# Moving the first two conversions of channel weights to the sixth and seventh round of the mixing

## The chip, the cores and the metric

The kernel runs on one core of one Trainium2 chip. Its time is the device time of one execution in microseconds (us); the figure quoted is the median of the runs. The core has five engines that each work through their own list of instructions in order: TensorE (PE in the profile, with its weight loads as PEld), VectorE (DVE), ScalarE (ACT), GpSimd (POOL) and SyncE (SP). SP here issues nearly all transfers (DMA). Engines wait for one another by semaphores. Nothing is reordered at run time, so an instruction that waits holds up all that stand behind it on its engine.

## The reference

The program is three stages in a row: a bucketed attention, a gated product, and a mixing block. The change lies in the third, which computes, for a batch of 2 with 768 positions and 512 channels:

```python
def _moe2_ref(x, w_ch1, w_ch2):
    X = np.fft.fft(x, axis=1)
    X = np.fft.fft(X, axis=2)
    mixed = np.real(X).astype(np.float32)
    u = x + mixed
    mu = np.mean(u, axis=-1, keepdims=True)
    var = np.mean((u - mu) ** 2, axis=-1, keepdims=True)
    un = (u - mu) / np.sqrt(var + 1e-06)
    ch = np.maximum(un @ w_ch1, 0.0) @ w_ch2
    return (u + ch).astype(np.float32)

def reference(**kwargs):
    ...
    attn_out = _attn_ref(**attn_kwargs)
    x = attn_out.transpose(0, 2, 1, 3).reshape(B, S, H * D)
    x = _moe_ref(x=x, **moe_kwargs)
    return _moe2_ref(x=x, **moe2_kwargs)
```

`w_ch1` is 512 x 2048 and `w_ch2` is 2048 x 512, both stored as 64-bit floats.

## The kernel before

The three stages run one after the other on the core: the attention until about 258 us, the gated product until about 284 us, the mixing until about 361 us, and the channel stage (the two products with `w_ch1` and `w_ch2`) to the end. Every fp32 operand of a product is split into a high and a low part, and three products take the place of one.

**The mixing** is the loop at L1201. Its 12 jobs are (batch, half, tile) of 128 positions: two batches, three tiles, two halves (s = 0 the even or cosine part, s = 1 the odd or sine part). The loop runs 14 rounds with i = 0 to 13, and is a software pipeline of three steps:

- `own` (L1100) multiplies job i by `w_out`: 12 matmuls of 512 columns, L1105.
- `along_d` (L1138) multiplies job i-2, turned, by the table of the transform along the channels: L1145, six matmuls of 258 columns, or eight for a cosine part (two of them with `first`). ScalarE copies the sum out (L1148, high part), and VectorE subtracts (L1149, low part).
- `turn` (L1122) transposes the folded job i-1 on TensorE, two transposes (L1126), or three for a cosine part (L1128); ScalarE copies them out (L1133, `ft`), VectorE subtracts (L1134).
- `fold` (L1113) copies job i out of its bank on ScalarE (L1115, `y`) and folds it on VectorE (L1118).

A job with s = 1 and tile 0 has two spans, and is turned and multiplied twice. The first product along d of a round reads the `ft` that ScalarE and VectorE made in the round before. In rounds 0 to 4 the second batch's even and odd parts are also formed (L1002, L1007, L1010). In round 7 `both` (L1180) finishes the first batch: `mixed` (L1151) multiplies the sums by the tables along the positions (L1165, 66 matmuls for a batch), VectorE adds (L1171 to L1176), and POOL forms u (L1186). A half's `mixed` reads the three slots of the sums of its half, high parts first. Rounds 8 to 10 center two tiles of u each on VectorE (`center`, L941, three instructions a tile: L944, L945, L946), and rounds 11 to 13 transpose two tiles each (`u_transpose`, L955: eight transposes of TensorE, two copies of ScalarE, two subtractions of VectorE, L962). After the loop `both` finishes the second batch, and the channel stage follows.

**The channel weights** come as 32 blocks of 128 x 512 64-bit floats, numbered h. `channel_load(h)` (L920) issues the DMA of a block on SP into one of two raw buffers. `channel_split(h)` (L935) converts a block into a high and a low fp32 part by `from64` (L128): VectorE L140, ScalarE L143, VectorE L146, L147, L150 and L151, ScalarE L155, POOL L156 (low part) and ScalarE L163 (high part). These steps form a chain that passes to and fro between the engines. Behind it `channel_split` issues the load of block h+2 into the raw buffer that it has just read. Blocks 0 and 1 are loaded in round 4 of the program's order. Blocks 2 and up are converted in the channel stage (L1259 and L1307 on).

The order on each engine is the order in which the Python code calls the instructions; there is no planner. So where a call stands in the loop decides behind what its instructions wait on VectorE, ScalarE and POOL.

Of the kernel before, what the change touches and what calls it, by code (L numbers as in the profile page):

```python
# [102 lines left out]
def block_kernel(  # L103
# [24 lines left out]
    def from64(words_of, raw, dst_h, dst_l, half=False, parts=P, spare=False):  # L128

        n = raw.shape[1]  # L130
        words = raw.bitcast(I32).rearrange("p (n two) -> p n two", two=2)
        lo, hi = words[:, :, 0], words[:, :, 1]
        a, e, g = (words_of(n, x)[:parts] for x in "aeg")
        b = 4 if half else 3

        def fold(x):
            return x.rearrange("p (c f) -> p c f", c=dst_h.shape[1]) if len(dst_h.shape) == 3 else x

        def s0():
            nc.vector.tensor_scalar(a, hi, 0x7FFFFE00, None, op0=ALU.bitwise_and)  # L140

        def s1():
            nc.scalar.activation(a, a, AF.Relu, scale=8.0, bias=col[:parts, b : b + 1])  # L143

        def s2():
            nc.vector.tensor_scalar(g, hi, 0x1FF, 15, op0=ALU.bitwise_and, op1=ALU.logical_shift_left)  # L146
            nc.vector.scalar_tensor_tensor(g, lo, 17, g, op0=ALU.logical_shift_right, op1=ALU.bitwise_or)  # L147

        def s3():
            nc.vector.scalar_tensor_tensor(a, hi, -(2 ** 31), a, op0=ALU.bitwise_and, op1=ALU.bitwise_or)  # L150
            nc.vector.tensor_scalar(e, a, -(2 ** 23), None, op0=ALU.bitwise_and)  # L151

        def s4():
            if spare:
                nc.scalar.mul(g.bitcast(F32), g, 2.0 ** -35)  # L155
                nc.gpsimd.tensor_tensor(dst_l, fold(g.bitcast(F32)), fold(e.bitcast(F32)), op=ALU.mult)  # L156
            else:
                nc.vector.scalar_tensor_tensor(
                    dst_l, fold(g), 2.0 ** -35, fold(e.bitcast(F32)), op0=ALU.mult, op1=ALU.mult
                )  # L160

        def s5():
            nc.scalar.copy(dst_h, fold(a.bitcast(F32)))  # L163

        return [s0, s1, s2, s3, s4, s5]
# [4 lines left out]
    def run(steps):  # L170
        for x in steps:
            x()
# [747 lines left out]
    def channel_load(h):  # L920

        if h >= 2 * NF:
            return
        f, i = divmod(h, 2)
        fs = slice(f * P, (f + 1) * P)
        r = wraw[h] = wq.tile([P, DM], I64, tag=f"raw{i}", name="raw")
        if i:
            nc.sync.dma_start(r, w_ch2[fs, :])
        else:
            nc.sync.dma_start(r.rearrange("p (c f) -> p c f", c=NC), w_ch1[:, fs].rearrange("(c p) f -> p c f", p=P))  # L930
# [4 lines left out]
    def channel_split(h):  # L935
        if h < 2 * NF:
            f, i = divmod(h, 2)
            run(from64(channel_words, wraw[h], *wch[f][2 * i : 2 * i + 2], spare=True))
            channel_load(h + 2)
# [24 lines left out]
    def mixing(es):  # L964
# [33 lines left out]
        def even_odd(b, c, pv_=None):  # L998

            back = g[b][:, c, S:HS:-1] if pv_ is None else pv_[:, ::-1]  # L1000
            for s in range(2):
                nc.vector.tensor_tensor(  # L1002
                    gts[(s + 2 * c) % len(gts)], g[b][:, c, 0:HS], back, op=ALU.subtract if s else ALU.add
                )

        def part_high(b, s, c):
            nc.scalar.copy(gh[b, s][:, c, :], gts[(s + 2 * c) % len(gts)])  # L1007

        def part_low(b, s, c):
            nc.gpsimd.tensor_tensor(  # L1010
                gl[b, s][:, c, :], gts[(s + 2 * c) % len(gts)], f32(gh[b, s])[:, c, :], op=ALU.subtract
            )
# [87 lines left out]
        def own(b, s, kt):  # L1100
            yp = psum()
            n = 0
            for x, w in ((gh[b, s], wo_h), (gh[b, s], wo_l), (gl[b, s], wo_h)):
                for c in range(NC):
                    nc.tensor.matmul(  # L1105
                        yp, x[:, c, kt * P : (kt + 1) * P], w[c], start=n == 0, stop=n == 3 * NC - 1
                    )
                    n += 1
            return yp
# [3 lines left out]
        def fold(b, s, kt, yp):  # L1113
            y = ys[b, s, kt] = m2.tile([P, DM], F32, tag="y", name="y", bufs=7)
            nc.scalar.copy(y, yp)  # L1115
            for part in (s,) if s == 0 or kt else (0, 1):
                fo = folds[b, s, kt, part] = m2.tile([P, 2 * P], F32, tag="fold", name="fold", bufs=2)
                nc.vector.tensor_tensor(  # L1118
                    fo, yp[:, 1:257], y[:, 511:255:-1], op=ALU.subtract if part else ALU.add
                )  # L1120

        def turn(b, s, kt, part):  # L1122
            n = 2 if part else 3
            pt = bank()
            for i, x in enumerate([folds[b, s, kt, part][:, i * P : (i + 1) * P] for i in range(2)]):
                nc.tensor.transpose(pt[:, i * P : (i + 1) * P], x, ident)  # L1126
            if n == 3:
                nc.tensor.transpose(pt[:, 2 * P : 3 * P], ys[b, s, kt][:, 0:P], ident)  # L1128
            fh, fl = turned[b, s, kt, part] = [
                m2.tile([P, 3, P], F32R, tag=f"f{x}", name="ft", bufs=2)[:, :n] for x in "hl"  # L1130
            ]
            src = pt[:, : n * P].rearrange("p (n t) -> p n t", n=n)
            nc.scalar.copy(fh, src)  # L1133
            nc.vector.tensor_tensor(fl, src, f32(fh), op=ALU.subtract)  # L1134
# [3 lines left out]
        def along_d(b, s, kt, part):  # L1138
            fh, fl = turned[b, s, kt, part]
            ops = [(x[:, i, :], tab[:, part, w, i, :]) for x, w in ((fh, 0), (fh, 1), (fl, 0)) for i in range(2)]  # L1140
            if part == 0:
                ops += [(x[:, 2, :], first) for x in (fh, fl)]
            pa = psum()
            for n, (x, w) in enumerate(ops):
                nc.tensor.matmul(pa[:, :NL], x, w, start=n == 0, stop=n == len(ops) - 1)  # L1145
            ah, al = sums[b]
            slot = kt if part == s else 3
            nc.scalar.copy(ah[:, part, slot, :], pa[:, :NL])  # L1148
            nc.vector.tensor_tensor(al[:, part, slot, :], pa[:, :NL], f32(ah)[:, part, slot, :], op=ALU.subtract)  # L1149
# [30 lines left out]
        def both(b, kt):  # L1180

            pm = [mixed(b, s, kt) for s in range(2)]
            for s in range(2):
                total(b, s, kt, pm[s])
            for t, op in ((kt, ALU.add), (3 + kt, ALU.subtract)):
                nc.gpsimd.tensor_tensor(u[b][:, t, :], ys[b, 0, kt], ys[b, 1, kt], op=op)  # L1186
# [10 lines left out]
        def spans(job):  # L1197
            b, s, kt = job
            return [(b, s, kt, part) for part in ((s,) if s == 0 or kt else (0, 1))]

        for i in range(len(jobs) + 2):  # L1201
            if i < len(jobs):
                yp = own(*jobs[i])
            if i > 1:
                for x in spans(jobs[i - 2]):
                    if x[0] not in sums:
                        sums[x[0]] = [m2.tile([P, 2, 4, NL], F32R, tag=y, name="a") for y in ("ah", "al")]
                    along_d(*x)
            if 0 < i <= len(jobs):
                for x in spans(jobs[i - 1]):  # L1210
                    turn(*x)
            if i == 7:
                both(0, 0)
                both(0, 1)
            if i < len(jobs):
                fold(*jobs[i], yp)
            if 0 < i < 5:
                for s in range(2):
                    part_high(1, s, i - 1)
                    part_low(1, s, i - 1)  # L1220
            if i < 4:
                even_odd(1, i)
            elif i == 4:
                gs.close()
                late_tiles()
                channel_load(0)
                channel_load(1)
            elif i == 7:
                both(0, 2)
            elif 8 <= i < 11:  # L1230
                for t in (i - 8, i - 5):
                    center(0, t)
                if i > 8:
                    channel_split(i - 9)
            elif i > 10:
                for x in range(2):
                    u_transpose(0, 2 * (i - 11) + x, psum)
# [3 lines left out]
    with ExitStack() as es:  # L1241
        mixing(es)
# [125 lines left out]
```

## Time and profile before

| | us |
|---|---|
| median of 3 runs | 638.09 (637.91 to 639.32) |
| the profiled execution, its own time | 639.26 |
| span of the profiled execution, first to last instruction | 637.5 |
| busy in the span: TensorE matmul | 618.5 (97%) |
| busy in the span: VectorE | 446.6 (70%) |
| busy in the span: ScalarE | 356.6 (56%) |
| busy in the span: POOL | 263.6 (41%) |
| mean granted TensorE clock (1 is full) | 0.995 |

The rows below are of that profiled execution; all times in them count from the start of its span. Busy matmul time is modelled, as matmuls are pipelined. The granted clock is the share of full speed that the chip allowed TensorE. A timeline row has the start, the duration, the engine, the line and the operation, output before input; in square brackets stands how long the engine was idle before it, and which engine's work ended that idle time. The chain of waits follows the work that ended last backwards, at each step to what released it.

### The profile page before, as it was taken

How to read it: one execution, taken by the hardware profiler on the slowest of the kernel's cores; microseconds unless marked ns; L12 is line 12 of the kernel's file. 1: busy time of each engine (PE TensorE's matmuls, PEld its weight loads, DVE VectorE, ACT ScalarE, POOL GpSimd, SP SyncE). 2: the span in 40 equal slices, each digit the busy share in tenths (PEclk: the TensorE clock that was granted, in tenths of full speed). 3: DMA queues.
4: the chain of work that ended last, by engine and by line, in shares of the span. 5: the costliest groups of instructions: out<-in, count | busy, mean ns of one | idle time of the engine just before them, and what ended most of it. 6: DMA issues, size and time to landing. Idle time of an engine off the chain costs nothing.

```text
span 637.5 us, 10561 instructions
## 1 busy us (share of the span) xinstructions
PE 618.5 (97%) x3794; PEld 578.1 (91%) x3794; DVE 446.6 (70%) x847; ACT 356.6 (56%) x713; POOL 263.6 (41%) x289
## 2 busy tenths in 40 slices
PE   7999999999999999999996999999999999999997
PEld 6899999999999998998895889999998999999996
DVE  4998989898989997897468788888885511111113
ACT  5887989898988897735325255555665110111221
POOL 7133577777888697873141433333331000000000
PEclk9999999999999999999998999999999999999999
DMA  6957475747747520261002044443440200000002
GB/s 155 197 127 178 117 185 125 163 121 161 169 117 184 145 65 10 70 244 48 0 2 67 1 133 133 132 133 122 125 130 21 100 1 1 0 1 1 1 1 99
DMA packets 54060, 60.25 MB, mean 95 GB/s; under 512 B 28936, under 2 KB 42332, under 8 KB 53752
## 3 DMA queue, kind: packets, MB, share of 16 engines
q1 hardware_dynamic: 53272, 56.02, 33.5%
q0 software_dynamic: 432, 3.55, 1.5%
q8 instruction: 30, 0.49, 0.3%
q14 instruction: 22, 0.18, 0.1%
q10 hardware_dynamic: 304, 0.01, 0.0%
HBM read 33.98 MB, written 3.15 MB: 58 GB/s over the span
## 4 chain that ended last, share of the span: by engine, by line
PE 86%; DVE 8%; ACT 2%; issue 1%; DMA 1%; POOL 0%; SPq 0%; DVEq 0%; ACTq 0%; POOLq 0%
PE pf L1275 20%; PE acc L1287 20%; PE sp L537 10%; PE op L597 9%; PE ptp L574 8%; PE ps L1105 4%; PE ps L216 3%; PE ps L1165 3%; PE bp L414 2%; PE ps L1145 2%; DVE ptl L586 2%; DVE sd L549 2%; PE late L216 1%; PE ptp L669 1%; PE ptp L649 1%
## 5 line engine op out<-in xcount | busy, mean ns | idle before, releaser
L1287 PE MATMUL acc<-w,hid 128*128 128x512 f32 x576 | 137.0, 390 | 0.0
L1287 PEld LDWEIGHTS acc<-w,hid 128*128 128x128 f32 x576 | 107.4, 188 | 19.7
L1278 DVE SCALAR_TENSOR_TENSOR hid<-pf,hid 128x384 fp32r<-128x384 f32 x60 | 32.3, 556 | 120.0 <-ACT hid L1277 120.0
L549 DVE TENSOR_SCALAR_CACHE_REDUCE sd<-sp 128x768 f32<-128x768 f32 x96 | 91.0, 949 | 14.7 <-PE sp L537 13.8
L1275 PE MATMUL pf<-uth,w 128*128 128x384 f32 x480 | 94.7, 338 | 0.3 <-POOL w L156 0.3
L586 DVE TENSOR_TENSOR ptl<-ptp,pth 128x768 fp32r<-128x768 f32 x96 | 91.5, 953 | 3.2 <-ACT pth L582 3.2
L537 PE MATMUL sp<-qk 128*128 128x384 f32 x384 | 90.9, 359 | 2.8 <-DVE sd L549 1.7
L582 ACT CAST pth<-ptp 128x768 fp32r<-128x768 f32 x96 | 77.3, 806 | 26.8 <-PE ptp L574 10.0
L556 ACT ACTIVATE sd<-sd,nm 128x768 f32<-128x768 f32 x96 | 90.7, 945 | 2.7 <-DVE sd L549 2.7
L1277 ACT ACTIVATE hid<-pf 128x384 fp32r<-128x384 f32 x60 | 28.0, 488 | 113.8 <-PE pf L1275 113.8
L1275 PEld LDWEIGHTS pf<-uth,w 128*128 128x128 f32 x480 | 85.6, 187 | 3.1 <-POOL w L156 0.6
L156 POOL TENSOR_TENSOR w<-cv 128x512 fp32r<-128x512 f32 x32 | 41.3, 1292 | 99.8 <-DVE cv L151 86.8
L574 PE MATMUL ptp<-ident,sd 128*128 128x128 f32 x576 | 78.6, 272 | 0.2 <-ACT sd L556 0.2
L597 PE MATMUL op<-ptl,v 128*128 128x256 f32 x288 | 73.6, 285 | 0.3 <-DVE ptl L586 0.3
L597 PE MATMUL op<-pth,v 128*128 128x256 f32 x288 | 73.5, 281 | 0.2 <-ACT xc L610 0.2
L537 PEld LDWEIGHTS sp<-qk 128*128 128x128 f32 x384 | 62.4, 189 | 6.5 <-DVE sd L549 4.3
L574 PEld LDWEIGHTS ptp<-ident,sd 128*128 128x128 f32 x576 | 65.9, 141 | 1.1 <-ACT sd L556 0.5
L615 POOL TENSOR_TENSOR xm<-xc,xs 64x256 f32<-64x256 f32 x48 | 35.5, 741 | 70.7 <-DMA xs<-xc 28.9
L597 PEld LDWEIGHTS op<-ptl,v 128*128 128x128 f32 x288 | 54.1, 188 | 1.7 <-DVE ptl L586 0.5
L597 PEld LDWEIGHTS op<-pth,v 128*128 128x128 f32 x288 | 54.1, 188 | 0.5 <-ACT xc L610 0.4
L143 ACT ACTIVATE cv<-cv,col 128x512 int32<-128x512 int32 x32 | 23.2, 725 | 53.5 <-DVE cv L140 53.5
L1275 PE MATMUL pf<-utl,w 128*128 128x384 f32 x240 | 52.1, 338 | 0.0
(214 smaller groups left out, 1050.7 us busy)
## 6 DMA issues: line engine op xcount, KB each, us to landing
raw<-in_moe_w_ch_dram SPq DMA_DIRECT2D x32, 512.0 KB
qk<-ht SPq DMA_DIRECT2D x60, 192.0 KB
qk<-lt SPq DMA_DIRECT2D x30, 192.0 KB
rqk<-in_q_dram SPq DMA_DIRECT2D x16, 192.0 KB
rqk<-in_k_dram SPq DMA_DIRECT2D x16, 192.0 KB
rv<-in_v_dram SPq DMA_DIRECT2D x8, 384.0 KB
out_dram<-o SPq DMA_DIRECT2D x12, 256.0 KB
xs<-xc SPq DMA_DIRECT2D x47, 64.0 KB
```

Source lines behind the costliest of these rows:

```text
L156: nc.gpsimd.tensor_tensor(dst_l, fold(g.bitcast(F32)), fold(e.bitcast(F32)), op=ALU.mult)
L537: nc.tensor.matmul(sp[:, a, :HS], q2[i][:, m, qi * P : (qi + 1) * P], k2[i][:, m, a * HS : (a + 1) * HS], start=m == 1, stop=m == 0,)
L549: nc.vector.tensor_scalar(sd[n].rearrange("p (a c) -> p a c", a=2), sp[:, :, :HS], CLAMP, None, op0=ALU.min, op1=ALU.min, accum_out=st[p][ ...
L556: nc.scalar.activation(sd[n], sd[n], AF.Exp, bias=st[p]["nm"][:, i : i + 1], scale=-1.0, accum_out=st[p]["sums"][:, i : i + 1],)
L574: nc.tensor.transpose(tp[:, r // 3, c0 : c0 + P], sd[n][:, r * P : (r + 1) * P], ident)
L582: nc.scalar.copy(p_parts(n)[0], tp)
L586: nc.vector.tensor_tensor(lo, tp, f32(ho), op=ALU.subtract)
L597: nc.tensor.matmul(po[kb], v3[:, r, c0 : c0 + P], pt[kb][x][:, r, :], start=r == 0 and x == 0, stop=r == R - 1 and x == 1,)
L615: add[kb] = lambda: nc.gpsimd.tensor_tensor(st[p]["xm"][mr, blk * QB : (blk + 1) * QB], xc[mr, :], xs[mr, :], op=ALU.add)
L1275: nc.tensor.matmul(pf[:, :HS], w[:, c, :], x[:, c, cs], start=n == 0, stop=n == 3 * NC - 1)
L1278: nc.vector.scalar_tensor_tensor(hl[:, cs], pf[:, :HS], 0.0, f32(hh)[:, cs], op0=ALU.max, op1=ALU.subtract)
L1287: nc.tensor.matmul(acc, x[:, ts_], w, start=f == 0 and n == 0, stop=f == NF - 1 and n == 2)
```

## The change

Two lines leave the branch for rounds 8 to 10, in which rounds 9 and 10 converted blocks 0 and 1, and a branch for rounds 5 and 6 is added that converts the same two blocks. Both places are at the end of their round.

```diff
--- before.py
+++ after.py
@@ -1230,8 +1230,8 @@
             elif 8 <= i < 11:
                 for t in (i - 8, i - 5):
                     center(0, t)
-                if i > 8:
-                    channel_split(i - 9)
+            elif 5 <= i < 7:
+                channel_split(i - 5)
             elif i > 10:
                 for x in range(2):
                     u_transpose(0, 2 * (i - 11) + x, psum)
```

Nothing else differs. The matmuls on TensorE and the DMAs on SP stand in the same order as before.

ScalarE, rounds 5 to 7, as a difference (the three added rows are one conversion; `cv` is its scratch, `w_0_4335` and `w_0_4337` are high parts of the channel weights, `ft` the turned job, `a` the sums, `y` the job):

```order
 L1133 CAST ft<-pw 128x384
 L1115 COPY y<-ps 128x512
+L143 ACTIVATE cv<-cv,col 128x512
+L155 ACTIVATE cv<-cv 128x512
+L163 CAST w_0_4335<-cv 128x512
 L1148 CAST a<-ps 128x258
 L1133 CAST ft<-pw 128x256
 L1115 COPY y<-ps 128x512
+L143 ACTIVATE cv<-cv,col 128x512
+L155 ACTIVATE cv<-cv 128x512
+L163 CAST w_0_4337<-cv 128x512
 L1148 CAST a<-ps 128x258
```

The two conversions now stand behind the copy `y` of rounds 5 and 6, and ahead of the copies of the sums and of `ft` of the next round.

ScalarE, rounds 9 to 11, as a difference:

```order
 L1133 CAST ft<-pw 128x384
 L1115 COPY y<-ps 128x512
-L143 ACTIVATE cv<-cv,col 128x512
-L155 ACTIVATE cv<-cv 128x512
-L163 CAST w_0_4335<-cv 128x512
 L1148 CAST a<-ps 128x258
 L1133 CAST ft<-pw 128x256
 L1115 COPY y<-ps 128x512
-L143 ACTIVATE cv<-cv,col 128x512
-L155 ACTIVATE cv<-cv 128x512
-L163 CAST w_0_4337<-cv 128x512
```

The copies of the sums and of `ft` of rounds 10 and 11 now follow the copy `y` of the round before directly.

VectorE at the end of round 9, as a difference (`mu_4323` and `u_4322` are the mean and the u of the first batch, `raw` the block as loaded):

```order
 L945 BN_AGGR mu_4323<-st 128x2
 L946 TENSOR_SCALAR u_4322<-u_4322,mu_4323 128x512
-L140 TENSOR_SCALAR cv<-raw 128x512
-L146 TENSOR_SCALAR cv<-raw 128x512
-L147 SCALAR_TENSOR_TENSOR cv<-raw,cv 128x512
-L150 SCALAR_TENSOR_TENSOR cv<-raw,cv 128x512
-L151 TENSOR_SCALAR cv<-cv 128x512
 L1149 TENSOR_TENSOR a<-ps,a 128x258
 L1134 TENSOR_TENSOR ft<-pw,ft 128x256
```

Behind the centering of the second tile of the round now stands the low part of the sums of round 10, with no conversion between. On POOL the two products L156 move ahead of the additions L1186 that form u for the first batch.

## Rows read from the trace of the kernel before

**Rows 1.** The page's slices, 15.9 us each: TensorE's granted clock in tenths, and bytes moved.

```profile
PEclk9999999999999999999998999999999999999999
...
GB/s 155 197 127 178 117 185 125 163 121 161 169 117 184 145 65 10 70 244 48 0 2 67 1 133 133 132 133 122 125 130 21 100 1 1 0 1 1 1 1 99
```

**Rows 2.** Waits, 323 to 362 us: who <- for whom, total us, times, longest us.

```profile
PE ps L1145 <- ACT ft L1133: 5.1, 2, 4.5
```

**Rows 3.** Stretches: length, busy us (count) of PE, PEld, DVE, ACT, POOL, then clock.

```profile
344.00:348.00 4.00, 1.16 (x5) 1.16 (x6) 3.37 (x8) 3.66 (x8) 1.28 (x1) 0.59 0.34 118
348.00:350.00 2.00, 2.00 (x11) 2.00 (x10) 1.66 (x4) 1.00 (x3) 0.00 (x0) 0.50 0.10 35
350.00:352.00 2.00, 2.00 (x13) 2.00 (x13) 1.25 (x3) 1.17 (x2) 0.00 (x0) 0.62 0.00 0
```

**Rows 4.** Chain of waits, 280 to 380 us: start, us, what; around the removed conversions.

```profile
330.48 1.71 PE ps L1145 x14
...
332.62 0.43 DVE a L1149
333.05 0.56 DVE ft L1134
...
333.96 0.61 DVE st L944
...
336.65 0.34 DVE cv L140
...
346.84 2.09 PE ps L1145 x8
...
352.92 7.97 PE ps L1165 x66
```

**Rows 5.** The same chain: TensorE's pieces at full clock.

```profile
306.45 0.72 PE ps L1145 x6
307.18 0.22 PE pw L1126 x2
...
307.50 2.81 PE ps L1105 x12
310.31 0.98 PE ps L1145 x8
...
352.05 0.87 PE ps L958 x8
```

**Rows 6.** Timeline, rounds 5 to 7: start, us, engine, line, operation; idle before it.

```profile
308.54 0.42 DVE L1118 TENSOR_TENSOR fold<-ps,y 128x256 f32<-128x256 f32 x1
...
311.32 0.38 ACT L1148 CAST a<-ps 128x258 fp32r<-128x258 f32 x1 [2.81 <-PE ps L1145]
...
312.50 0.42 DVE L1118 TENSOR_TENSOR fold<-ps,y 128x256 f32<-128x256 f32 x1
...
315.07 0.38 ACT L1148 CAST a<-ps 128x258 fp32r<-128x258 f32 x1 [2.60 <-PE ps L1145]
...
316.54 1.26 PE L1165 MATMUL ps<-a,seq 128*128 128x258 f32 x9
...
318.54 0.42 DVE L1171 TENSOR_TENSOR y<-y,ps 128x257 f32<-128x257 f32 x1 [1.06 <-PE ps L1165]
```

**Rows 7.** Timeline: first conversion in round 9, its start and what follows it.

```profile
336.56 0.42 DVE L140 TENSOR_SCALAR cv<-raw 128x512 int32<-128x512 int32 x1
...
339.21 0.37 ACT L1148 CAST a<-ps 128x258 fp32r<-128x258 f32 x1
339.25 1.27 POOL L156 TENSOR_TENSOR w<-cv 128x512 fp32r<-128x512 f32 x1 [11.79 <-DVE cv L151]
```

**Rows 8.** Timeline of SP's queue: issue of the first two raw channel blocks.

```profile
284.25 0.38 SPq L930 DMA_DIRECT2D raw<-in_moe_w_ch_dram  x1
284.68 0.51 SPq L928 DMA_DIRECT2D raw<-in_moe_w_ch_dram  x1
```

**Rows 9.** Timeline, round 11: the pair of VectorE's subtractions for u.

```profile
347.80 1.29 DVE L962 TENSOR_TENSOR utl<-ps,uth 128x512 fp32r<-128x512 f32 x2
```

## The prediction

> **What bounds the kernel now.** I read the profile in this order: the slices of the page, the table of waits for the stretch around the removed conversions, the stretch table with the granted clock, the chain of waits, and the timeline of the rounds that lose or receive a conversion. Round i below is the pass with that index of the mixing loop (i counts from 0, so the change's sixth, seventh, tenth and eleventh rounds are 5, 6, 9 and 10). TensorE is the bound nearly everywhere; the reader is to see the one place where it is not. In the page's slices its clock shows one dip, in the slice that begins near 335 us [rows 1]. The waits of 323 to 362 us put 5.1 us of TensorE's idleness on two waits of L1145 (the products along d) for ScalarE's L1133, 4.5 us of it in one piece [rows 2]. The granted clock then stands at 0.59 in 344 to 348 us and at 0.50, the lower level of 1.2 GHz, in 348 to 350, and averages 0.62 over 350 to 352, so that it is full again only near the end of that stretch [rows 3]. The chain of waits says why: from 332 to 347 us it leaves TensorE and runs through VectorE's products, folds and centerings into the first conversion, on into a further round of the same and into the second conversion, and returns at 346.84 [rows 4]. So the two conversions lie on the path that sets the end, in rounds in which VectorE is already full: without one, round 9 takes VectorE 4.03 us (332.62 to 336.65, [rows 4]), while TensorE needs 2.81 + 0.98 + 0.22 = 4.01 us for a round of one `own`, eight products and two turns [rows 5].
>
> **What is removed from rounds 9 and 10.** A conversion is five VectorE, three ScalarE and one POOL instruction and, behind them, one load issued by SP. From its first instruction at 336.56 to ScalarE's next copy for the mixing at 339.21 it holds that chain for 2.65 us [rows 7]. Nothing in these rounds covers it. What comes next when it is gone has to be followed on both engines, in the chain's times.
>
> TensorE: the products of round 9 end at 330.48 + 1.71 = 332.19 [rows 4]. A turn with three transposes takes 0.32 (307.18 to 307.50), so `own` of round 10 starts at 332.51; 2.81 for it, 0.98 for eight products and 0.22 for a turn of two put round 11 at 336.52. From there at full clock: `own` 2.81, six products 0.72, a turn 0.32, eight transposes of u 0.87, which ends at 341.24; eight products 0.98, a turn 0.22, u 0.87, to 343.31; six products 0.72 and u 0.87 [rows 5]. With no wait the second batch's `mixed` starts at 344.90.
>
> VectorE: round 9 ends at 336.65 as before. Round 10 waits for its products (336.30) and ScalarE's copy of them, about 0.4, so it runs from 336.7 for 4.03, to 340.7. Round 11 is 0.43 + 0.56 + 0.42 and the pair of u subtractions, 1.29 [rows 4, 6, 9], to 343.4; the low parts of the last turn follow 0.43 + 0.56 later, at 344.4. The last six products read them from their fifth matmul, at 343.31 + 4 x 0.12 = 343.8. So about 0.5 us of wait is left, and `mixed` starts at 345.4 instead of 352.92 [rows 4]: **7.5 us** gained. A second route gives the same: 5.1 us of waits [rows 2], plus what the slow clock took, which is 352.92 - 346.84 = 6.08 us for work of 0.98 + 0.22 + 0.87 + 0.72 + 0.87 = 3.66 us at full clock, 2.4 us; together 7.5. Bounds: 8.0 if VectorE never holds TensorE (344.90), and 6.5 if handovers and the trailing VectorE cost another microsecond. I take 7.5.
>
> **What is added to rounds 5 and 6.** Here VectorE has no centering, and from round 5 on no even and odd parts. ScalarE stood idle for 2.81 us ahead of the copy at 311.32 and 2.60 us ahead of the one at 315.07 [rows 6]; this idle time is the cover. In round 5 VectorE is free at 308.54 + 0.42 = 308.96; 2.65 us later, at 311.61, ScalarE turns to the copy that ran at 311.32, 0.29 us late. TensorE's next use of that round's turn is a whole `own` (2.81) later. In round 6 the fold of 312.50 moves to 312.79, VectorE is free at 313.21, and the copy of 315.07 runs at 315.86, ending at 316.24 (it takes 0.38), with VectorE's subtraction ending near 316.7. This is the tight place: `mixed` of the sine half starts at 316.54 and reads the copied slot in its third matmul, at 316.54 + 2 x 0.14 = 316.82, and the low part in its seventh, at 317.38 [rows 6]. 0.6 us of slack remain, so I cost this at nothing; without the cover each conversion would cost up to 2.65 us. VectorE's additions behind it come 0.5 us late and recover in the idle 1.06 us ahead of 318.54 [rows 6]. POOL's two products (1.27 each, [rows 7]) end near 317.2, before the sums for u that start when VectorE's additions are through.
>
> **Loads.** The two raw blocks that the moved conversions read were issued at 284.25 and 284.68 us [rows 8], and the slices show the core's transfers at 0 and 2 GB/s between 303 and 335 us [rows 1], so they have long landed at 308. The loads that each conversion issues behind it move with it, to about 311 and 316, into that quiet stretch and past no other entry of SP's queue; their first reader is the third conversion, behind the mixing. Cost nothing.
>
> **After the mixing.** The third conversion and the first channel matmul are released by the last VectorE addition of the mixing, as before. Everything from `mixed` of the second batch on is tied to that point and not to a fixed time, so the gain should reach the end whole.
>
> **The sum.** The profiled execution took 639.26 us, span 637.5; minus 7.5 that is 631.8, span 630.0. The median of the runs shown is 638.09, 1.17 below the profiled one. Against it: 638.09 - 7.5 = **630.6**.
>
> **Rivals.** (a) *VectorE stays the bound to the end of the rounds.* Its round 12 with u is 0.43 + 0.56 + 1.29 = 2.3 us against TensorE's 2.07, and round 13 is alike; if each handover is 0.2 late and the waits grow to 1.5 to 3 us in rounds 11 to 13, the gain is 5 to 6.5: 631.6 to 633.1. For it: 4.03 against 4.01 leaves no reserve. Against it: round 11 gives VectorE time, since TensorE has 4.7 us there.
>
> (b) *The clock falls anyway.* From 339.3 to the start of `mixed` TensorE would run 5.6 us, of which 3.2 are transposes (three times 0.87, 0.32, 0.22). If such a mix did not hold the clock, up to 5.6 us would be lost again: 636.2. Against it: the clock rose from 0.50 in 348 to 350 us to a mean of 0.62 over 350 to 352, so full by its end, while TensorE ran this very mix of products and u transposes [rows 3]. The Trainium skill, in TensorE: Matmul & The Clock Gate, section Part 4: PE-mode transpose, says that transposes do not count as activity that brings the full clock. By that rule alone the time would lie towards 636; the trace speaks against it as far as these two microseconds go.
>
> (c) *The stall is moved, not removed, and the program becomes slower.* The place is the third matmul of the sine half at 316.82. It decides when the copy of 315.86 comes more than 0.6 us later than I have it. Exposed in full, the two conversions cost 2 x 2.65 = 5.3; if the clock fell there too, the 66 matmuls of `mixed` (7.97 us, [rows 4]) would run at half speed and cost up to 8.0 more. 638.09 - 7.5 + 13.3 = 643.9. The stall alone, without the clock, still leaves a gain: 635.9. It needs both, and ScalarE's idle times speak against either.
>
> (d) *Nothing changes*, because what is won in the mixing is waited for at the start of the channel stage: it would need a transfer or POOL step there that is tied to an absolute time, and I see none. 638.
>
> **How the numbers follow.** The forecast, 630.6 with 629.8 to 631.6 for its own bounds, gets 0.78; (a) 0.10; (b) 0.03; the stall of (c) without the clock 0.02; (c) in full 0.03; (d) 0.04. A difference of 0.2%, 1.3 us, is about what a measurement of this kernel tells from no change. Faster is the forecast, (a), (b) and the half of (c): 0.93; same 0.04; slower 0.03. The range holds the forecast and (a), with some room above for handovers: 629.6 to 633.1.
>
> **What would show it.** Right: L1145 in rounds 11 and 12 no longer waits for L1133; the clock shows no dip in any slice; the second batch's `mixed` starts near 345.4; ScalarE's copies of 311.32 and 315.07 come 0.3 and 0.8 us later and TensorE does not notice; the stretch from `mixed` to the end is as long as before. Wrong: a wait of L1165 for L1148 near 317, a clock dip near 317 or 345, or a new wait at the first channel matmuls.

## The result, and the profile after

The changed kernel takes 631.44 us (631.11 to 631.64, 4 runs) against 638.71 us (637.91 to 639.64, 4 runs) of the kernel before: the ratio is 0.9884, with a 95% interval of 0.9872 to 0.9897, so 7.3 us are gained, 6.6 to 8.2 by the interval. The forecast was 638.09 - 7.5 = 630.6; the difference predicted, 7.5 us, is met within 0.2, and the median lies 0.8 us above the forecast mostly because the median of before was 0.6 us higher this time: its four runs are two pairs, 637.91 and 638.09, 639.32 and 639.64, and the median lies between them. The profiled execution of the changed kernel took 631.46 us. Its trace runs ahead of the trace of before by 0.12 us at the start of round 5 (303.53 against 303.65) and by 0.13 us where `mixed` of the first batch begins (315.23 against 315.36); 0.13 us is to be added to its times where the two are set side by side.

The page of the changed kernel: span, and the granted clock in slices.

```profile
span 629.7 us, 10559 instructions
...
PEclk9999999999999999999999999999999999999999
```

The span is 629.7 us against 637.5, and the slice with the dip of the clock [rows 1] is gone: all 40 stand at 9 tenths or more.

The table of waits of the changed kernel, from 316 us to the first rounds of the channel stage; some of TensorE's rows: who <- for whom, total us, times, longest us.

```profile
PE acc L1275 <- DVE y L1176: 0.9, 1, 0.9
...
PE acc L1275 <- ACT w L163: 0.6, 1, 0.6
...
PE acc L1275 <- POOL w L156: 0.3, 1, 0.3
PEld ps L1145 <- DVE ft L1134: 0.2, 1, 0.2
```

The 5.1 us of L1145 waiting for ScalarE's L1133 [rows 2] are no longer there. What is left of waits in the mixing is a weight load (PEld) that waits 0.2 us for VectorE's low part L1134. The three rows of L1275 belong to the start of the channel stage; the longest of them, 0.9 us for the last addition, was there before too.

The stretches of the changed kernel; the columns are as in [rows 3].

```profile
340.00:344.00 4.00, 3.97 (x35) 3.74 (x33) 3.93 (x9) 3.90 (x9) 0.00 (x0) 1.00 0.00 0
344.00:346.00 2.00, 2.00 (x19) 2.00 (x19) 1.87 (x5) 1.45 (x3) 0.00 (x0) 1.00 0.00 0
346.00:348.00 2.00, 2.00 (x19) 2.00 (x19) 1.30 (x4) 0.00 (x0) 0.00 (x0) 1.00 0.00 0
```

TensorE is busy for 3.97 of 4.00 us in 340 to 344 and the clock is at 1.00 throughout, where before it stood at 0.59, 0.50 and 0.62 [rows 3]. VectorE is no less busy than before in that stretch (3.93 of 4.00): it is full, but almost nothing waits for it.

The chain of waits of the changed kernel through rounds 11 to 13 and the second batch's `mixed`.

```profile
339.17 0.72 PE ps L1145 x6
...
340.22 0.87 PE ps L958 x8
341.09 1.05 PE ps L1145 x8
...
343.24 0.48 PE ps L1145 x4
...
343.75 0.51 PE ps L1145 x2
...
345.13 7.99 PE ps L1165 x66
...
353.15 0.42 DVE y L1171
```

It stays on TensorE from one end to the other, but for a break of 0.03 us ahead of the last two products of round 13. In the chain of before the same addition of VectorE stands here:

```profile
360.91 0.42 DVE y L1171
```

`mixed` of the second batch begins at 345.13, 345.26 in the time of before, against 352.92 [rows 4]: 7.7 us earlier. It takes 7.99 us as before (7.97), and from VectorE's addition at 353.15 to the end of the span are 629.7 - 353.15 = 276.6 us, as before (637.5 - 360.91 = 276.6). Nothing of the gain is lost behind it.

The timeline of the changed kernel in rounds 5 to 7, where the conversions are now.

```profile
311.41 0.37 ACT L1148 CAST a<-ps 128x258 fp32r<-128x258 f32 x1
...
315.56 0.36 ACT L1148 CAST a<-ps 128x258 fp32r<-128x258 f32 x1
...
316.40 1.26 PE L1165 MATMUL ps<-a,seq 128*128 128x258 f32 x9
```

ScalarE's copies L1148 come at 311.41 and 315.56; in the time of before these are 311.54 and 315.69, so they are 0.22 and 0.62 us later than at 311.32 and 315.07 [rows 6]. The sine half starts at 316.40, and TensorE has no wait there. The load behind the second conversion goes out at 315.02, in the quiet stretch.

### The profile page after: what moved, and what is told of

Same layout as the page of the kernel before. It is cut to its first block, busy times and chain, and to the rows that moved or that the text cites. A ratio compares the mean times of both kernels' runs of the same rounds, so it can differ in the third digit from the quotient of the medians.

```text
span 629.7 us, 10559 instructions
## 1 busy us (share of the span) xinstructions
PE 616.0 (98%) x3794; PEld 576.7 (92%) x3794; DVE 445.9 (71%) x847; ACT 356.4 (57%) x713; POOL 263.9 (42%) x289
## 4 chain that ended last, share of the span: by engine, by line
PE 88%; DVE 7%; ACT 2%; issue 1%; DMA 1%; POOL 0%; SPq 0%; DVEq 0%; ACTq 0%; POOLq 0%
PE pf L1275 20%; PE acc L1287 20%; PE sp L537 10%; PE op L597 9%; PE ptp L574 8%; PE ps L1105 5%; PE ps L216 3%; PE ps L1165 3%; PE bp L414 2%; PE ps L1145 2%; DVE ptl L586 2%; DVE sd L549 2%; PE late L216 1%; PE ptp L669 1%; PE ptp L649 1%
## 5 line engine op out<-in xcount | busy, mean ns | idle before, releaser
L1275 PE MATMUL pf<-uth,w 128*128 128x384 f32 x480 | 94.8, 338 | 0.2 <-POOL w L156 0.2
L1275 PEld LDWEIGHTS pf<-uth,w 128*128 128x128 f32 x480 | 85.7, 188 | 2.9 <-POOL w L156 0.6
L156 POOL TENSOR_TENSOR w<-cv 128x512 fp32r<-128x512 f32 x32 | 41.4, 1294 | 89.6 <-DVE cv L151 76.6
L1275 PE MATMUL pf<-utl,w 128*128 128x384 f32 x240 | 52.1, 338 | 0.0
```

The source lines that it names most:

```text
L1275: nc.tensor.matmul(pf[:, :HS], w[:, c, :], x[:, c, cs], start=n == 0, stop=n == 3 * NC - 1)
```

## Experiments

Two theories besides mine were set against each other. **A**: the conversions lay on the chain of VectorE and ScalarE for which TensorE waits, in rounds that VectorE already fills, and the slow clock followed from the wait. **B**: the gain comes from weights and loads being there earlier. **C**: only ScalarE's place behind the conversion matters, not VectorE's work. In the kernels that add lines the line numbers behind them shift by a few; L1145 and L1165 are named by their operation where that happens.

### Only the first conversion moved

```diff
                 for t in (i - 8, i - 5):
                     center(0, t)
-                if i > 8:
-                    channel_split(i - 9)
+                if i == 10:
+                    channel_split(1)
+            elif i == 5:
+                channel_split(0)
```

> Block 0 is converted in round 5, block 1 stays in round 10. Theory A (the two conversions lay on the chain of VectorE and ScalarE that TensorE waits for, in rounds that VectorE fills already, and the slow clock followed from the long wait): round 10 of VectorE ends near 340.5 as in the changed kernel, the conversion then holds ScalarE's next copies to about 343.1, so the products of round 12 wait some 2.8 us instead of 4.5, and there is no wait of 0.6 us in round 11. Gain 4.7 us against the kernel before if the clock stays at full, 3 if it falls. Theory B (the gain comes from weights and loads being there earlier): each block carries its half, gain 3.7, with no link to a wait of L1145. Nothing of the computation is left out.

Measured: 635.68 us, ratio 0.9955 (0.9941 to 0.9970), a gain of 2.7 us. TensorE's timeline around round 12 of this kernel:

```profile
343.93 1.39 PE L1145 MATMUL ps<-tab,ft 128*128 128x258 f32 x6 [2.73 <-ACT ft L1133]
```

the stretch behind it:

```profile
344.00:348.00 4.00, 4.00 (x20) 3.95 (x21) 3.28 (x7) 2.76 (x7) 0.48 (x1) 0.57 0.30 115
```

and the start of `mixed` in its chain:

```profile
349.54 8.00 PE ps L1165 x66
```

The wait is the 2.73 us that theory A gave (2.8), behind the turned sine part, and the clock fell after it, to 0.57 in 344 to 348 us. The 3 us forecast for that case were nearly met. Against the changed kernel 2.73 us of wait are lost, and 1.6 us in the work behind it, a part of which ran at the lower clock: from 343.93 to `mixed` at 349.54 are 5.61 us, where the changed kernel takes 345.13 - 341.09 = 4.04. Theory B gave 3.7 for this half, and it names no such wait.

### Only the second conversion moved

```diff
                 for t in (i - 8, i - 5):
                     center(0, t)
-                if i > 8:
-                    channel_split(i - 9)
+                if i == 9:
+                    channel_split(0)
+            elif i == 6:
+                channel_split(1)
```

> Block 1 is converted in round 6, block 0 stays in round 9. Theory A: the wait of 0.6 us in round 11 and the short one behind it stay, VectorE is 2.65 us late through round 10 and ends it near 343.5, the low parts of the last cosine turn come near 344.5, and the products of round 12 wait 1.5 to 2 us for them, with the clock at full. Gain about 5 us against the kernel before; together with the run that moves block 0 alone more than the 7.3 of both, since the two delays add up on one chain. Theory B: gain 3.7, and the two runs add up to 7.3.

Measured: 633.75 us, ratio 0.9923 (0.9906 to 0.9939), a gain of 4.6 us. TensorE's two waits, and the clock in the stretch behind them:

```profile
339.51 1.03 PE L1145 MATMUL ps<-tab,ft 128*128 128x258 f32 x6 [0.59 <-ACT ft L1133]
...
343.94 0.50 PE L1145 MATMUL ps<-tab,ft 128*128 128x258 f32 x2 [1.52 <-DVE ft L1134]
```

```profile
344.00:348.00 4.00, 4.00 (x34) 3.92 (x35) 3.88 (x9) 2.98 (x7) 0.00 (x0) 1.00 0.02 4
```

The 0.59 us of round 11 are back as in the kernel before, and in round 12 TensorE stops at the fifth of six matmuls for 1.52 us, for VectorE's low part of `ft`, as forecast; the clock stays at 1.00. So one conversion too many in round 9 is felt two rounds later, through VectorE. One expectation failed: the two runs were to add up to more than 7.3 us, and they give 2.7 + 4.6 = 7.3, the sum that theory B had given. I had left out of that sentence that the first of them loses part of its gain to the clock. Against theory B speak the unequal halves, and that the changed kernel takes the same 276.6 us as before from VectorE's addition to the end: nothing was won where the weights are read.

### Both conversions left in rounds 9 and 10, ahead of the centerings

```diff
             elif 8 <= i < 11:
-                for t in (i - 8, i - 5):
-                    center(0, t)
                 if i > 8:
                     channel_split(i - 9)
+                for t in (i - 8, i - 5):
+                    center(0, t)
```

> Both conversions stay in rounds 9 and 10, but stand ahead of the centerings of the round and no longer behind them. Theory A: VectorE has 4.03 + 2.65 us of work in such a round in either order, against 4.0 of TensorE, so the waits change their place (from ScalarE's L1133 to VectorE's low parts, L1134) and are split into several of 0.5 to 2.6 us, 5 us together; the clock may hold, since no single wait is as long as 4.5. Gain 0 to 3 us. Theory C (it is only ScalarE's place behind the conversion that holds TensorE, not VectorE's work): ScalarE is through with its part while VectorE centers, and the gain is 5 us or more.

Measured: 637.92 us, ratio 0.9990 (0.9981 to 1.0000), 0.4 us or nothing. TensorE's waits in this kernel, and its clock:

```profile
340.15 0.50 PE L1145 MATMUL ps<-tab,ft 128*128 128x258 f32 x2 [0.43 <-DVE ft L1134]
...
343.78 0.74 PE L1145 MATMUL ps<-tab,ft 128*128 128x258 f32 x4 [1.82 <-ACT ft L1133]
346.81 0.80 PE L1145 MATMUL ps<-tab,ft 128*128 128x258 f32 x2 [2.29 <-DVE ft L1134]
```

```profile
344.00:348.00 4.00, 1.71 (x9) 1.51 (x9) 3.93 (x9) 1.19 (x3) 0.33 (x1) 0.61 0.29 108
```

The two waits of before, 0.60 and 4.50 us, are now three, 0.43, 1.82 and 2.29 us, 4.5 us together (I had said 5), two of them for VectorE's L1134. ScalarE's copy `ft` of round 11 ends at 343.73 instead of 346.78, 3 us earlier, and it helps nothing, since TensorE then stops until 346.81 for VectorE's low part, as late as before (346.84): theory C falls. The order within the round matters little, the amount of VectorE work in it does. The clock, which I thought might hold, fell to 0.61 in 344 to 348 us, so that little of the 3 us that were possible remained.

### The kernel before, with TensorE kept busy in the wait

```diff
         for i in range(len(jobs) + 2):
             if i < len(jobs):
                 yp = own(*jobs[i])
+            if i == 12:
+                to = psum()
+                for _ in range(30):
+                    nc.tensor.matmul(to[:, :NL], gh[1, 0][:, 0, 0:P], first, start=True, stop=True)
```

> The kernel before with 30 further products of 258 columns at the start of round 12, 3.6 us at full clock, into a bank that nobody reads, in the 4.5 us in which TensorE waited there. They are added work that changes no output. Theory A: TensorE has hardly any idle time left there, the granted clock stays at 1.00 in 344 to 352 us, and the 2.4 us that the slow clock took come back: 636.3 us. If the slow clock costs nothing, or falls all the same: 638.7. That tells how the 7.3 us divide into waits (5.1) and clock (2.4).

Measured: 637.10 us, ratio 0.9982 (0.9972 to 0.9991), a gain of 1.2 us, 0.6 to 1.8 by the interval. The added matmuls and the rest of the wait in the timeline:

```profile
341.79 3.85 PE L1207 MATMUL ps<-first,gh 128*128 128x258 f32 x30
346.53 1.10 PE L1145 MATMUL ps<-tab,ft 128*128 128x258 f32 x6 [0.90 <-ACT ft L1133]
```

The chain from there to `mixed`:

```profile
346.53 1.34 PE ps L1145 x8
...
349.50 0.51 PE ps L1145 x2
...
350.88 8.00 PE ps L1165 x66
```

The clock in the stretches that were slow before:

```profile
344.00:348.00 4.00, 3.10 (x25) 2.84 (x24) 3.41 (x7) 3.66 (x9) 1.28 (x1) 1.00 0.44 129
348.00:350.00 2.00, 1.96 (x17) 1.75 (x16) 2.00 (x6) 1.63 (x4) 0.00 (x0) 1.00 0.01 4
```

The clock stays at 1.00, and the products start where they started before (346.53 is 346.83 in the time of that trace). From there to `mixed` are 350.88 - 346.53 = 4.35 us, against 352.92 - 346.84 = 6.08 before [rows 4]. So the clock cost 1.7 us in the trace, where I had put 2.4. The difference (4.35 against the 3.66 that I had counted) falls into two: the first eight products take 1.34 us behind the wait, not 0.98, and with TensorE fast again the last six wait for VectorE's low parts, which the slow clock had covered (the last two take 0.51 us as in the changed kernel). The median gives still less, 1.2, and the interval just reaches 1.7. The runs of before differ among themselves, too: in 12 of the 19 in this series the mean granted clock is 0.997 and the median time 638.25 us, in 6 it is 0.995, as in the profiled execution, and the median 638.97; the run here lies 1.15 and 1.87 us below these. So what the clock costs differs from run to run. That the clock share is some 1 to 2 us, and the greater part of the gain is the waits, is shown; its exact size is not.

### Each conversion done twice in rounds 5 and 6

On the changed kernel:

```diff
             elif 5 <= i < 7:
+                channel_split(i - 5, False)
                 channel_split(i - 5)
```

Here `False` leaves out the load behind the first of the two.

> The changed kernel with each of the two conversions done twice in its round (5 and 6), the same result written again; the added work changes no output. Theory A (the place in rounds 5 and 6 is free because ScalarE and VectorE have 2.6 to 2.8 us of idle time there and no more; I left 0.6 us of slack in round 7): the second conversion of a round has no cover and also waits for POOL's L156 of the first. TensorE waits 1 to 2 us for L1133 ahead of the products of round 7 and 3 to 5 us in mixed ahead of the sine half, and the clock may fall there: 631.4 + 5 to 9 = 636.5 to 640.5. Rival D (VectorE and ScalarE have far more room there than my 0.6 us, or TensorE does not depend on them so soon): 631.4 to 632.5.

Measured: 640.49 us, against 638.9 us of before on the same chip, ratio 1.0030 (1.0019 to 1.0041); so 9 us more than the changed kernel, at the upper end of what was expected, and slower than the kernel before. The second conversion on VectorE, POOL's product ahead of it, and TensorE's two waits (the lines of the mixing are one higher here):

```profile
311.06 1.29 POOL L156 TENSOR_TENSOR w<-cv 128x512 fp32r<-128x512 f32 x1 [4.49 <-DVE cv L151]
311.15 1.49 DVE L140 TENSOR_SCALAR cv<-raw 128x512 int32<-128x512 int32 x1 [0.23 <-ACT w L163]
...
315.55 1.02 PE L1146 MATMUL ps<-tab,ft 128*128 128x258 f32 x6 [1.76 <-ACT ft L1134]
...
323.28 1.47 PE L1166 MATMUL ps<-a,seq 128*128 128x258 f32 x7 [3.38 <-ACT a L1149]
```

The clock in two stretches behind the waits:

```profile
316.00:320.00 4.00, 3.89 (x21) 3.41 (x19) 3.44 (x8) 1.86 (x3) 1.10 (x2) 0.62 0.37 121
...
324.00:326.00 2.00, 2.00 (x11) 2.00 (x11) 0.86 (x3) 0.00 (x0) 0.19 (x1) 0.50 0.53 203
```

The waits are 1.76 us ahead of the products of round 7 (forecast 1 to 2) and 3.38 us in `mixed` ahead of the third matmul of the sine half, for ScalarE's copy, at the place that the prediction had called the tight one. The clock fell after both, to 0.62 and 0.50. The waits make 5.1 of the 9 us; the rest, of which the slower work behind them is likely a part, was not divided further. So the room in rounds 5 and 6 is real but fits one conversion, not two: rival D falls, and so does the idea that the place in the order hardly matters.

### The first channel matmuls in another pair of banks

The trace of the changed kernel leaves 0.94 + 0.56 + 0.32 us of waits at the start of the channel stage. This is its timeline there: POOL's u, TensorE's first channel matmuls, two instructions of the third conversion, and TensorE's two waits for `w`.

```profile
350.52 6.62 POOL L1186 TENSOR_TENSOR u<-y 128x512 f32<-128x512 f32 x5
...
354.05 1.64 PE L1275 MATMUL acc<-uth,w 128*128 128x384 f32 x8 [0.94 <-DVE y L1176]
354.48 1.51 DVE L146 TENSOR_SCALAR cv<-raw 128x512 int32<-128x512 int32 x1
...
356.03 1.67 DVE L147 SCALAR_TENSOR_TENSOR cv<-raw,cv 128x512 int32<-128x512 int32 x1
...
359.05 0.96 PE L1275 MATMUL acc<-uth,w 128*128 128x384 f32 x4 [0.56 <-ACT w L163]
...
360.33 0.97 PE L1275 MATMUL acc<-uth,w 128*128 128x384 f32 x4 [0.32 <-POOL w L156]
```

The edit, on the changed kernel:

```diff
-            pf = tile_a(2 + 2 * g + a) if g < 2 else tile_f()
+            pf = tile_a(2 + 2 * g + a) if g == 1 else tile_f()
```

> The changed kernel; the first channel matmuls go into the two banks of the pair pf and no longer into acc2 and acc3, so they do not wait for the last addition of the mixing (0.94 us in both kernels). Theory E (the path at that point runs from that addition through the third conversion to w of L1275, and not through TensorE): TensorE starts 0.9 us earlier and waits that much longer for w: 631.4, within 0.3. Rival F (each wait of TensorE counts): 630.5.

Measured: 631.56 us (631.46 to 631.69), ratio to before 0.9886: as the changed kernel.

```profile
352.93 1.56 PE L1275 MATMUL pf<-uth,w 128*128 128x384 f32 x8
...
359.06 0.96 PE L1275 MATMUL acc<-uth,w 128*128 128x384 f32 x4 [1.77 <-ACT w L163]
```

TensorE starts at 352.93 instead of 354.05 and then waits 1.77 us instead of 0.56; it resumes at 359.06 and 360.33, within 0.01 us of where it did. A wait that is not on the path is worth nothing (theory E).

### The VectorE part of the third conversion in round 7

On the changed kernel; `split_front` is `channel_split` up to the scaling of the low word, with the load, and `split_back` the copy and POOL's product of the same block:

```diff
             elif i == 7:
                 both(0, 2)
+                split_front(2)
...
-        channel_split(2)
+        split_back(2)
```

> The changed kernel with the VectorE part and the scaling of the third conversion in round 7, behind both for the first batch, where VectorE stood idle for 2.9 us and ScalarE for 4.6; only the copy and POOL's product of it stay at the start of the channel stage. By the same reasoning as for the first two: covered in round 7 (cost 0), and the waits of 0.56 and 0.32 us of L1275 for w go: 631.4 - 0.9 = 630.5; the 0.94 us behind the last addition stay. If round 7 has no cover, the products of round 8 or 9 wait instead and the time is 631.4 or more.

Measured: 630.51 us (630.19 to 631.58), ratio to before 0.9868: 0.9 us below the changed kernel, as forecast; with the interval, 0.9852 to 0.9885 against 0.9872 to 0.9897, the difference is not clear of the noise. The profiled execution is the slowest of the four (631.58 us). At the start of the channel stage it is about 1.6 us later than the changed kernel: 1.15 us of them it has already at the first batch's `mixed` (316.14 against 314.99), ahead of the moved work. TensorE in round 12 and at the start of the channel stage:

```profile
343.12 0.52 PE L1169 MATMUL ps<-tab,ft 128*128 128x258 f32 x2 [0.39 <-DVE ft L1158]
...
355.63 1.64 PE L1300 MATMUL acc<-uth,w 128*128 128x384 f32 x8 [0.94 <-DVE y L1200]
...
359.91 1.56 PE L1300 MATMUL acc<-uth,w 128*128 128x384 f32 x8
```

The 0.94 us stay, the two waits for `w` are gone. But the cost in round 7 is not 0: TensorE waits 0.39 us in round 12 for VectorE's low part (L1158 here), and the time between the two `mixed` grows by 0.4 us, from 29.90 (314.99 to 344.89) to 30.31 (316.14 to 346.45). In turn the start of the channel stage, from that `mixed` to the first product with `w_ch2`, takes 17.65 us instead of 19.01, 1.4 less, more than the 0.9 of idle time. The forecast of 0.9 was met by two errors that offset each other.

### Both edits

> Both edits. TensorE starts the channel stage 0.94 us earlier and finds w ready or nearly (POOL is busy with u until about 357 and forms the low part then, ready near 358.4, while TensorE wants it near 357.9): 631.4 - 0.9 - 0.5 = 630.0, and 629.5 if both gains are whole. By rival F with the other two runs: the two gains add up.

Measured: 629.63 us (629.17 to 629.92), ratio to before 0.9855 (0.9841 to 0.9870). This beats both kernels: 9.3 us below the runs of before on its chip, and 1.8 us below the changed kernel's median. The forecast was 630.0, and 629.5 if both gains were whole.

```profile
352.81 1.56 PE L1300 MATMUL pf<-uth,w 128*128 128x384 f32 x8
...
357.01 1.92 PE L1300 MATMUL acc<-uth,w 128*128 128x384 f32 x8
```

The four first blocks of channel matmuls follow one another without a wait. The wait in round 12 is here too (0.38 us). The edit of the banks, worth nothing alone, is worth 0.9 us once the wait for `w` behind it is gone.

## Why the prediction was right

**The bound.** That the two conversions were on the path, in rounds that VectorE fills, was read from the chain of waits. The runs show it from three sides: moving either one brings its own part (2.7 and 4.6 us), changing the order within the round brings next to nothing, and taking away the clock's part alone leaves most of the loss.

**The gain, 7.5 us forecast.** The trace gives 7.7 at the start of `mixed`, the runs 7.3. That the two lie within 0.2 us of the forecast is in part luck, as the runs of before differ by more than that among themselves (637.91 to 639.64); what is shown is the path. Step by step: round 11 was put at 336.52 and its products along d ended at 339.17 + 0.72 = 339.89, or 340.02 in the time of before (forecast 340.05); the u transposes of that round ended at 341.09 (341.22; forecast 341.24). For the last six products I expected a wait of 0.5 us for VectorE's low part (0.6 by the prediction's own figures, 344.4 - 343.8); there the chain shows a break of 0.03 us and two matmuls that take 0.51 instead of 0.24, 0.3 us together. That is the 0.2 us by which the trace beat the forecast. The prediction took 0.56 us for VectorE's low part of that turn; it takes 0.41, as this turn has two blocks and not three.

**The division.** The term that was mis-sized is the slow clock in the second route: 2.4 us, where the run that keeps TensorE busy shows 1.7 in the trace and 1.2 in the median. The sum of the route came out right because another term was too small. The products of round 12 start at 341.09, 341.22 in the time of before, against 346.84 [rows 4]: 5.6 us earlier, where the idle times were 5.1. So the two stops cost 0.5 us beyond their idle time; products behind a stop take longer than in a stream (eight of them 1.34 us and 0.98, in the run that keeps TensorE busy and in [rows 5]). From there to `mixed` are 4.04 us against 6.08, 2.0 us, since VectorE's lateness takes a part of what the clock gives back. 5.6 and 2.0 make the 7.7; that 5.1 and 2.4 came so near is luck. The first route, which followed both engines through the rounds, did not need that division.

**The cost of the new place, nothing forecast.** Right: 0.22 and 0.62 us of lateness (forecast 0.29 and 0.78). The second copy ends at 315.56 + 0.36 = 315.92, and the third matmul of the sine half comes at 316.40 + 2 x 0.14 = 316.68, so 0.76 us of slack were left (forecast 0.6). One reading is wrong without harm: with the high parts of three slots under two tables first, the low part of that slot is read by the ninth matmul, not the seventh, which leaves 0.3 us more. Rival (c) named the place where it would break, and the run with doubled conversions broke it there: 3.38 us at the third matmul of the sine half, and the clock with it.

**Rivals (a), (b) and (d).** VectorE held TensorE for about 0.3 us, in round 13. The clock held through 5.2 us of which 3.2 are transposes, from 339.89 to 345.13, at 1.00 in all stretches. By the rule in the Trainium skill, TensorE: Matmul & The Clock Gate, section Part 4: PE-mode transpose, such work would not count for the clock as other work does. This trace does not decide that: its transposes stand between products, at most 1.2 us of them in a row (339.89 to 341.09), and the clock also held after 1.52 us without any work (second conversion moved). And the channel stage, tied to the end of the mixing, kept its length.

## What to carry to other kernels

Before moving work off a full stretch, follow both the engine that waits and the engine that it waits for through the next rounds with the trace's own durations: here that gave the gain within 0.2 us, while counting waits alone would have missed what the clock costs and what the other engine still owes. The cover at the new place has a size, and one conversion per round was it: 2.6 to 2.8 us of idle time took 2.65 us of work, and twice that gave back all the gain. A wait next to the path is worth nothing until the one behind it is gone; mend the one on the chain first, then look again. And an engine that comes late into full rounds stays late: what the third conversion cost VectorE in round 7, TensorE waited for in round 12.

## What the runs showed of the hardware

**VectorE beside POOL.** In the changed kernel L146 takes 1.51 us and L147 1.67 at 354 to 358 us, while POOL runs its additions for u; alone they take 0.42 and 0.69 (rounds 5 and 6 of that kernel). The same happens in round 7 of the last kernel, where I had counted on 2.65 us:

```profile
324.11 2.83 POOL L1210 TENSOR_TENSOR u<-y 128x512 f32<-128x512 f32 x2 [0.31 <-DVE y L1200]
...
324.29 1.52 DVE L949 TENSOR_SCALAR cv<-raw 128x512 int32<-128x512 int32 x1
...
325.84 1.65 DVE L950 SCALAR_TENSOR_TENSOR cv<-raw,cv 128x512 int32<-128x512 int32 x1
```

and in the doubled one L140 takes 1.49 us beside POOL's L156. So the room in round 7 was less than I took it for, and the conversion did not quite fit: the 0.39 us in round 12 are what was left over. VectorE's additions L1171, which read a PSUM bank and one SBUF tile, keep their 0.42 us beside POOL. The Trainium skill, GPSIMD Engine Reference, section Key points, says that GpSimd shares its SBUF interfaces with VectorE, and that instructions with two SBUF inputs or in a two-port mode contend; L147, with two inputs from SBUF, agrees with that, and about 1 us for each of these instructions is the price here. L140 and L146 have one input; which mode they ran in, no run shows.

**The clock after short waits.** The granted clock fell to the lower level, 1.2 GHz, after an idle time of TensorE of 2.73 us (first conversion moved), and in the doubled kernel after one of 1.76 us; after 1.52 us in round 12 (second conversion moved) it stayed at 1.00. I had expected it to hold below the 4.5 us seen before. But the length of one idle time does not decide it: in the run with the other pair of banks alone it stayed at 1.00 after the 1.77 us ahead of 359.06.

```profile
356.00:360.00 4.00, 2.23 (x12) 1.61 (x10) 3.27 (x6) 2.02 (x4) 2.16 (x2) 1.00 0.08 13
```

What does decide it was not tried.
